# Moving PSUM reads of a soft-MoE kernel from VectorE to ScalarE, with the addition one block later

## The chip, the cores and the metric

The kernel runs on one core of a Trainium2 chip. The metric is the device time of one execution in microseconds. Three timed runs of the kernel before gave 395.83 (median), 395.76 and 396.35.

## The reference

Causal attention over 8 batches of 12 heads (448 positions, 64 channels each) is followed by a soft mixture of experts over all 3584 tokens of 768 channels. Cut to what matters:

```python
attn = softmax(where(causal, q @ k.T / 8, -1e9));  x = attn @ v      # per batch and head
x = x.transpose(0, 2, 1, 3).reshape(3584, 768)
logits = x @ phi                                  # 32 slots
d = exp(logits - logits.max(0));  d /= d.sum(0)   # softmax over the tokens
slot_input = d.T @ x                              # 32 x 768, "dispatch"
slot_out[e] = relu(slot_input[e] @ w1[e]) @ w2[e] # 8 experts of 4 slots
c = softmax(logits, axis=1);  out = c @ slot_out
```

The softmax of d runs over all tokens. So the kernel keeps a running maximum and a running sum over the batches, and rescales the summed slot input each time by a factor `al`.

## The kernel before, in words

The work is a loop over 48 pairs of heads (`block(p)`, p from 0 to 46, then `last_block`); six pairs make a batch. Every engine keeps the order in which the program issues its instructions (`_InOrder`, line 57). Because of that helper, all instructions of the profile stand under line 67, and one goes by the names of the tiles.

Scores need two passes. The first pass (`scores1_all`, lines 285 to 287) computes the transposed scores of one head into one of three PSUM score tiles `s_` (line 96; 128 partitions by 1024 columns of float32, which is two banks of 512 columns). Its first matmul writes the causal mask (`tri`) into columns 512 to 703. VectorE takes maxima over the scores (`max_keys`, `r<-s` and `r<-r`), TensorE transposes them (`max_row`, into `rt`, or for the second head of a pair into the last 128 columns of a score tile), VectorE reduces them to a row (`mr`), and GpSimd spreads it into an operand (`max_spread`, `r<-mr`). A second pass (`scores2`, `s<-r,k`) subtracts the maxima and adds the low parts of the operands; ScalarE takes exponentials of a whole tile (`exps`, `pt<-s`), and TensorE multiplies them by the values (`attv_pair`, `po<-va,pt`). VectorE divides by the sums (`norm`; its part 2, `x<-po,sm`, runs at the start of the next block), TensorE transposes x (`xtrans`) and ScalarE copies it out (`xcopy`).

The running mixture of experts is strewn over the blocks by the remainder p % 6 (`m6`), lines 645 to 673. At the end of a block the score tile of the pair's second head, `m = s_[(a + 1) % 3]` with a = 2 p, is free, and TensorE writes into it:

- in blocks with remainder 3, 5 and 1 the logits of a pair of head pairs (j = 0, 2, 4) into columns 0 to 127; `logits_t` (lines 444 to 446) adds them on VectorE to the tile `lt`. For j = 0 the second operand is `mk`, a constant that holds 0, and -1e30 where the batch has no tokens (448 of 512 rows are real);
- in remainder 2 the transposed weights and logits of the batch before, copied out by VectorE;
- in remainder 3, 4 and 0 (from p = 7 on) the products of a dispatch: 128 columns, 256 columns (both at column 512) and 384 columns (at column 0). `dispatch_b` (lines 486 to 489) rescales the running slot input `si` by `al` and adds the products in one VectorE instruction.

The transposed maxima of the next head go into columns 896 to 1023 of the same tile m, and their reduction `mr` precedes `logits_t` and `dispatch_b` on VectorE. Two score passes later, in the next block, the tile m takes the first-pass scores of head a + 4 (`scores1_all(a' + 2)` of the next block p + 1, a' = 2 p + 2). So its first matmul, the mask, has to wait until m has been read.

The order on each engine around the change of blocks is then: TensorE: attention times values, logits or dispatch, the transposed maxima, `xtrans`, the second pass of the next block's first head, the mask and the first pass into m, the second pass of the second head, the first pass of another head, attention times values. VectorE: `norm` parts 0 and 1 (`sm<-po` and the reciprocal `sm<-sm`), `mr`, `logits_t`, `dispatch_b`, `norm` part 2, then the maxima. ScalarE: casts of the operands, the factors of the running softmax (`al`, `lt<-run_m`, `run_z`), the next exponential.

After the attention the experts' weights, 50 MB in all of which a part is loaded ahead, are streamed through tiles that lie over dead tiles of the attention (`wt1`, line 781); a pad (`PAD`, lines 39 and 777) sets where they begin.

Of the kernel before, what the change touches and what calls it, by code (L numbers as in the profile page):

```python
# [9 lines left out]
F32 = mybir.dt.float32  # L10
F32R = mybir.dt.float32r
BF16 = mybir.dt.bfloat16
AF = mybir.ActivationFunctionType
ALU = mybir.AluOpType
# [3 lines left out]
P = 128  # L18
# [16 lines left out]
RES, TW1, LATE2 = 24, 11, 4  # L35

HT = 2
WN, PAD = 1536, 192
WARM = (2, 3, 3)
START = (9, 6, 2, 4)  # L40

# [41 lines left out]
def attention_soft_moe(ctx: ExitStack, tc: tile.TileContext, qk, va, phi, w, out):  # L83
    nc = _Core(tc)
    const = ctx.enter_context(tc.tile_pool(name="const", bufs=1, side="left"))
# [30 lines left out]
    ltn = moe.tile([P, P + 1], F32, name="lt")  # L116
    lt = ltn[:, 0:P]
    gs = moe.tile([P, P], F32, name="gs")
    mk = moe.tile([P, P], F32, name="mk")

    st = {"w": 0}
# [14 lines left out]
    def loads_v(p, eng=nc.sync):  # L136
        if p < NPAIR:
            eng.dma_start(out=va_[p % 2], in_=va[p])
# [30 lines left out]
    def load_w(n):  # L169
        if n < len(order):  # L170
            t = wtiles[order[n]] = slot(n, f"w{n}")
            q, g, c = place(n), (n + 2) // 4, WN * ((n + 2) % 4)
            if n < RES or n == NBUF or q >= RES + LATE2:
                nc.sync.dma_start(out=t, in_=w[g, :, c:c + WN])
            elif 4 <= q < RES and n > NBUF:
                if q % 4 == 3:
                    nc.sync.dma_start(out=group(n), in_=w[g])
            elif n % 2:
                t = group(n)
                nc.sync.dma_start(out=t[:, 2 * WN:] if q < RES else t, in_=w[g, :, c - WN:c + WN])  # L180
# [54 lines left out]
    def cast_q(p, hs=slice(0, 2)):  # L235
        if p < NPAIR:
            nc.scalar.activation(out=qd[:, hs], in_=st["raw", 0, p][:, hs], func=AF.Copy)
# [97 lines left out]
    def scores2(i, cs):  # L335
        if i >= NHD:
            return
        p, h = divmod(i, 2)
        s = st["s", i]
        k2 = k2_  # L340
        for c in cs:
            o, w, m = KS * h + P * c, S - CQ0[c], min(P, KS - P * c)
            nc.tensor.matmul(s[0:m, SCOL[c]:SCOL[c] + w], k2[:, o:o + m],
                             r2[:, h, CQ0[c]:S], start=False, stop=True, skip_group_check=True)

    def exps(i):
        if i < NHD:
            nc.scalar.activation(out=pt_[i % 2][:, 0:1024], in_=st.pop(("s", i)), func=AF.Exp, scale=SCALE)
# [49 lines left out]
    def x_of(p):  # L398
        if p % 3 == 0:
            xn = st["xn", p // 3] = x_[p // 3 % XB]  # L400
            for k in range(3):
                st["x", p + k] = xn[:, :, P * k:P * k + P]
        return st["x", p]

    def norm(p, k):
        if k == 0:
            sm = st["sm", p] = moe.tile([P, NQ], F32, tag="sm", name=f"sm{p}", bufs=2)
            nc.vector.tensor_scalar(out=sm, in0=po2[:, :, HD], scalar1=EPS, scalar2=None, op0=ALU.add)
        elif k == 1:
            nc.vector.reciprocal(out=st["sm", p], in_=st["sm", p])  # L410
        else:
            x, sm = x_of(p), st.pop(("sm", p))
            m = NCH - 1
            nc.vector.tensor_tensor(out=x[:, 0:m].rearrange("p c (h d)->p h c d", h=2),
                                    in0=po2[:, 0:2 * m, 0:HD].rearrange("p (h c) d->p h c d", h=2),
                                    in1=sm[:, 0:2 * m].rearrange("p (h c)->p h c", h=2).unsqueeze(3)
                                    .to_broadcast([P, 2, m, HD]), op=ALU.mult)
            for h in range(2):
                a = AW * h
                nc.vector.tensor_scalar(out=x[0:AW, m, HD * h:HD * h + HD], in0=po2[a:a + AW, 2 * m, 0:HD],  # L420
                                        scalar1=sm[a:a + AW, 2 * m:2 * m + 1], scalar2=None, op0=ALU.mult)
# [21 lines left out]

    def logits_t(j, g):

        nc.vector.tensor_tensor(out=lt, in0=g, in1=lt if j else mk, op=ALU.add)

    def logits_b(b):

# [36 lines left out]
    def dispatch_b(b, hf, sp, sl=slice(0, 384)):  # L486
        s = si[:, 384 * hf + sl.start:384 * hf + sl.stop]
        nc.vector.scalar_tensor_tensor(out=s, in0=s, scalar=st["al", b][:, 0:1], in1=sp[:, 0:sl.stop - sl.start],
                                       op0=ALU.mult, op1=ALU.add)
# [8 lines left out]
    phis = [const.tile([P, 3, NSLOT], F32, tag="ph", name=f"phi{hf}", bufs=2) for hf in range(2)]  # L498
    run_m = [const.tile([P, 1], F32, name=f"run_m{i}") for i in range(2)]
    run_z = const.tile([P, 1], F32, name="run_z")  # L500
    lg = const.tile([P, NB, NCH, NSLOT], F32, name="lg")


# [16 lines left out]
    copy_k2(0, h0)  # L520
    sub_k(0, h0, nc.vector)
    nc.vector.memset(pob, 0.0)
    for t, v in ((mk, 0.0), (mk[96:P, 64:P], -1.0e30), (ltn[:, P:P + 1], -1.0e30), (run_m[1], 1.0e30), (run_z, 0.0)):
        nc.vector.memset(t, v)
    sub_q(0, h0)
    scores1_all(0)
# [37 lines left out]
    def block(p):  # L564
        a, b = 2 * p, p // 6 - 1
        m6 = p % 6
        if p + 1 < NPAIR:
            loads_v(p + 1, nc.sync if p + 1 < NPAIR - 1 else nc.scalar)
        if p % 2 and p < 44 or p in (16, 30):
            load_w(st["w"])  # L570
            st["w"] += 1

        if p:
            norm(p - 1, 2)
        scores2(a, range(NCH))
        exps(a)
        if p == 0:
            copy_k2(0, h1)
            cast_q(1, h1)
            warm(START[3], pob)  # L580
            max_row(1, 0)
            max_row(1, 1)
            max_spread(1)
            sub_k(1, h1, nc.vector)
        elif p > 1:
            xcopy(p - 2)
            if p == NPAIR - 2:
                sub_q(p + 1, h0)
        scores1_all(a + 2)
        if p == 0:  # L590
            warm(START[2], pob)
        for k in range(3):
            max_keys(a + 2, k)
        if p == 0:
            cast_k(2, h0)
        scores2(a + 1, range(NCH))
        exps(a + 1)
        if p == 0:
            cast_k(2, h1)
        scores1_all(a + 3)  # L600
        if m6 == 2 and p > 6:
            logits_b(b)
        max_keys(a + 3, 0)
        late_k = p == 1
        if p == 1:
            sub_q(2, h0)
            sub_k(3, h0)
            sub_q(2, h1)
            load_qk(4, 0)
        elif p:  # L610
            sub_k(p + 2, h0 if late_k else slice(0, 2))
            if not late_k:
                load_qk(p + 4, 1)
            sub_q(p + 1, h1 if p == NPAIR - 2 else slice(0, 2))
            load_qk(p + 3, 0)
        else:
            sub_q(1, h0)
            sub_q(1, h1)
            load_qk(3, 0)
            sub_k(2, h0)  # L620
        copy_k2(p + 1)
        if m6 == 2 and p > 6:
            logits_d(b, lt)
        if p:
            cast_k(p + 3)
            cast_q(p + 2)
        else:
            cast_q(2)
            cast_k(3)
        if m6 == 3 and p > 6:  # L630
            logits_al(b)
        elif m6 == 4 and p > 6:
            logits_n(b)
        attv_pair(p)
        max_row(a + 2, 1)
        max_spread(a + 2)
        if p == 0:
            sub_k(2, h1)
            load_qk(4, 1)
        for k in (1, 2):  # L640
            max_keys(a + 3, k)
        for k in range(2):
            norm(p, k)

        m = s_[(a + 1) % 3]
        parts = []
        if m6 in (1, 3, 5) and p > 1:
            j = (m6 + 3) % 6
            logits_a(b if m6 == 1 else p // 6, (j, j + 1), m[:, 0:P])
        elif m6 == 2 and p > 6:  # L650
            logits_e(b, m, 0)
        if m6 == 3 and p > 6:
            parts = [(b, 0, slice(0, P), 512)]
        elif m6 == 4 and p > 6 and p < NPAIR - 2:
            parts = [(b, 0, slice(P, 3 * P), 512)]
        elif m6 == 0 and p > 6:
            parts = [(b - 1, 1, slice(0, 3 * P), 0)]
        for d, hf, sl, o in parts:
            dispatch_a(d, hf, m[:, o:o + sl.stop - sl.start], sl)
        max_row(a + 3, 0, to=m[:, 1024 - P:1024])  # L660
        max_row(a + 3, 1)
        if m6 == 2 and p > 6:
            logits_e(b, m, 1)
        max_spread(a + 3)
        if late_k:
            sub_k(p + 2, h1)
            load_qk(p + 4, 1)
        if m6 in (1, 3, 5) and p > 1:
            logits_t(j, m[:, 0:P])
        for d, hf, sl, o in parts:  # L670
            dispatch_b(d, hf, m[:, o:o + sl.stop - sl.start], sl)
        if p:
            xtrans(p - 1)

# [31 lines left out]
    for c in range(NCH):  # L706
        n = P if c < NCH - 1 else AW
# [207 lines left out]
    n = NBUF  # L915
# [93 lines left out]
```

## Time and profile before

| what | value |
|---|---|
| median of three timed runs | 395.83 us |
| the profiled execution's own time | 396.08 us |
| its span from first to last instruction | 394.4 us |
| granted TensorE clock, mean | 0.979 |
| attention loop, from the first exponential to the last | about 10 to 297 us |
| bytes moved | 119.17 MB, mean 302 GB/s |

The profile comes from one execution. Each row of a group gives the line, engine, operation, the tile written and the tiles read, the shapes, the count, busy time and mean duration of one. Rows of the timeline begin with the start and the duration in us, and end with the idle time of the engine before them and what ended it, where there was any. PE is TensorE's matmuls, PEld its weight loads, DVE VectorE, ACT ScalarE, POOL GpSimd, SP the queue that issues most DMAs. Ends of matmuls are modelled.

### The profile page before, as it was taken

To read this page: it belongs to the slowest core of one execution; us is meant where nothing else is said; L and a number is where in the kernel's file an instruction comes from. 1 tells how busy PE (TensorE), PEld (TensorE's weight loads), DVE (VectorE), ACT (ScalarE), POOL (GpSimd) and SP (SyncE) were. 2 spreads that over 40 slices of the span, in tenths; PEclk is the share of its full clock that TensorE was granted. 3 is DMA by queue.
4 is the path that set the end of the run, shared out by engine and by line. 5 is a ranking of instruction groups with operands and counts; after the bars stand their busy time and mean duration, and the time that the engine had idled before them with its cause. 6 is when DMAs were issued, how large, how long until landed. Compare 5 with 4: busy or idle time off the path is not lost.

```text
span 394.4 us, 13997 instructions
## 1 busy us (share of the span) xinstructions
PE 366.3 (93%) x5763; PEld 293.9 (75%) x5763; DVE 295.2 (75%) x835; ACT 282.9 (72%) x397; POOL 256.5 (65%) x215
## 2 busy tenths in 40 slices
PE   7899999999999999999999999999999989988940
PEld 3689889888988998898889888988986544533420
DVE  7887889888888888898888988888886675342550
ACT  5888899898898898888988988888864012431440
POOL 5998899898898888898988988889860000000000
PEclk9999999999999999999999999999999999998985
DMA  7868877788898788777997877887579999999996
GB/s 250 277 229 281 288 288 237 251 273 274 274 318 272 244 270 300 257 246 248 307 323 256 286 240 249 275 287 250 183 246 399 422 431 428 429 421 419 433 429 295
DMA packets 28720, 119.17 MB, mean 302 GB/s; under 512 B 3440, under 2 KB 3952, under 8 KB 26480
## 3 DMA queue, kind: packets, MB, share of 16 engines
q1 hardware_dynamic: 28512, 118.01, 83.2%
q8 instruction: 45, 0.74, 0.7%
q10 hardware_dynamic: 144, 0.27, 0.2%
q14 instruction: 19, 0.16, 0.1%
HBM read 107.25 MB, written 11.01 MB: 300 GB/s over the span
## 4 chain that ended last, share of the span: by engine, by line
PE 67%; DMA 9%; POOL 9%; DVE 5%; ACT 4%; issue 2%; SPq 0%; POOLq 0%; DVEq 0%; ACTq 0%
PE s L67 34%; PE po L67 20%; DMA w<-in_w_dram 8%; POOL r L67 6%; PE xm L67 4%; POOL ks L67 3%; PE so L67 2%; PE e L67 2%; PE pp L67 2%; PE rt L67 2%; DMA kraw<-in_qk_dram 1%; ACT qd L67 1%; DVE lm L67 1%; DVE lg L67 1%; ACT w L67 1%
## 5 line engine op out<-in xcount | busy, mean ns | idle before, releaser
L67 DVE TRANSPOSE_TENSOR_REDUCE r<-s 128x32 f32<-128x1024 f32 x96 | 119.5, 1245 | 7.7 <-PE s L67 4.9
L67 ACT ACTIVATE pt<-s 128x1024 f32<-128x1024 f32 x96 | 98.8, 1029 | 31.0 <-PE s L67 24.0
L67 PEld LDWEIGHTS po<-va,pt 128*64 128x64 f32 x3008 | 102.3, 138 | 11.8 <-issue 11.3
L67 PE MATMUL po<-va,pt 128*64 128x65 f32 x3008 | 109.2, 224 | 0.0
L67 POOL TENSOR_TENSOR r<-qraw,qd 64x896 fp32r<-64x896 f32 (+1 forms) x50 | 99.4, 1989 | 1.9 <-ACT qd L67 1.8
L67 POOL TENSOR_TENSOR ks<-kraw,ks 64x896 fp32r<-64x896 f32 (+1 forms) x48 | 89.7, 1870 | 4.1 <-ACT ks L67 0.5
L67 POOL TENSOR_SCALAR_AFFINE_SELECT r<-mr 14x448 fp32r<-14x448 f32 x96 | 61.6, 643 | 32.9 <-DVE mr L67 28.6
L67 PE MATMUL s<-qd,ks 128*66 128x64 f32 (+3 forms) x384 | 80.6, 321 | 0.0
L67 PE MATMUL s<-r,k 128*128 128x448 f32 (+3 forms) x384 | 65.2, 291 | 2.7 <-POOL r L67 2.7
L67 PEld LDWEIGHTS s<-r,k 128*128 128x128 f32 (+1 forms) x384 | 59.3, 176 | 8.6 <-POOL r L67 5.9
L67 PEld LDWEIGHTS s<-qd,ks 128*128 128x128 f32 (+1 forms) x384 | 52.5, 183 | 2.1 <-issue 0.9
L67 ACT ACTIVATE ks<-kraw 128x896 fp32r<-128x896 f32 (+1 forms) x49 | 45.0, 920 | 5.6 <-DMA kraw<-in_qk_dram 4.4
L67 ACT ACTIVATE k<-ks 64x896 fp32r<-64x896 f32 (+1 forms) x49 | 45.8, 936 | 1.2
L67 ACT ACTIVATE qd<-qraw 128x896 fp32r<-128x896 f32 (+1 forms) x48 | 44.6, 929 | 0.9 <-POOL r L67 0.7
L67 PE MATMUL s<-tri,identb 128*128 128x192 bf16 x192 | 39.6, 270 | 0.6
L67 DVE TENSOR_REDUCE r<-r 128x16 f32<-128x32 f32 x192 | 33.7, 176 | 5.0
L67 DVE TENSOR_REDUCE mr<-s 14x32 f32<-14x128 f32 x47 | 13.1, 279 | 21.4 <-ACT qd L67 14.8
L67 PE MATMUL xm<-ident,x 128*128 128x128 f32 x188 | 28.3, 273 | 0.0
L67 ACT ACTIVATE xts<-xm 128x512 f32<-128x512 f32 x46 | 27.2, 591 | 0.4 <-PE xm L67 0.4
L67 DVE TENSOR_SCALAR x<-po,sm 64x64 f32<-64x64 f32 x94 | 25.9, 276 | 0.7
L67 DVE COPY w<-pp 128x384 f32<-128x384 f32 x28 | 14.5, 553 | 15.4 <-PE pp L67 15.3
L67 DVE TENSOR_TENSOR x<-po,sm 128x384 f32<-128x384 f32 x47 | 25.2, 537 | 0.0
(151 smaller groups left out, 397.9 us busy)
## 6 DMA issues: line engine op xcount, KB each, us to landing
w<-in_w_dram SPq DMA_DIRECT2D x34, 768.0 KB, 6.7
kraw<-in_qk_dram SPq DMA_DIRECT2D x46, 448.0 KB, 4.4
qraw<-in_qk_dram SPq DMA_DIRECT2D x46, 448.0 KB, 4.5
w<-in_w_dram SPq DMA_DIRECT2D x5, 3072.0 KB, 25.0
va<-in_va_dram SPq DMA_DIRECT2D x47, 260.0 KB, 4.8
out_dram<-w SPq DMA_DIRECT2D x7, 1536.0 KB, 12.6
w<-in_w_dram SPq DMA_DIRECT2D x5, 1536.0 KB, 11.2
qk<-in_qk_dram SPq DMA_DIRECT2D x2, 448.0 KB, 7.1
```

The lines of the kernel that those rows point to most:

```text
L67: return self._tc.keep_in_program_order(op(*args, **kwargs))
```

## The change

For the first pair of a batch (j = 0) `logits_t` no longer adds a constant on VectorE; ScalarE copies the logits out of the score tile into `lt`. The -1e30 of the missing tokens is written into `lt` by VectorE in the next block (remainder 4). Of a dispatch of 256 or 384 columns VectorE sums only the first 128 out of PSUM. ScalarE copies the other 128 or 256 columns into a new buffer `scr` in SBUF, and VectorE sums that copy into `si` in the next block, behind the reciprocal. The constant `mk` is no longer filled at the start; the tile stays, since the tail uses it. The pad shrinks from 192 to 128 columns, and `scr` takes 256 columns.

```diff
--- before.py
+++ after.py
@@ -35,7 +35,7 @@
 RES, TW1, LATE2 = 24, 11, 4
 
 HT = 2
-WN, PAD = 1536, 192
+WN, PAD = 1536, 128
 WARM = (2, 3, 3)
 START = (9, 6, 2, 4)
 
@@ -443,7 +443,10 @@
 
     def logits_t(j, g):
 
-        nc.vector.tensor_tensor(out=lt, in0=g, in1=lt if j else mk, op=ALU.add)
+        if j:
+            nc.vector.tensor_tensor(out=lt, in0=g, in1=lt, op=ALU.add)
+        else:
+            nc.scalar.activation(out=lt, in_=g, func=AF.Copy)
 
     def logits_b(b):
 
@@ -498,6 +501,7 @@
     phis = [const.tile([P, 3, NSLOT], F32, tag="ph", name=f"phi{hf}", bufs=2) for hf in range(2)]
     run_m = [const.tile([P, 1], F32, name=f"run_m{i}") for i in range(2)]
     run_z = const.tile([P, 1], F32, name="run_z")
+    scr = const.tile([P, 2 * P], F32, name="scr")
     lg = const.tile([P, NB, NCH, NSLOT], F32, name="lg")
 
 
@@ -520,7 +524,7 @@
     copy_k2(0, h0)
     sub_k(0, h0, nc.vector)
     nc.vector.memset(pob, 0.0)
-    for t, v in ((mk, 0.0), (mk[96:P, 64:P], -1.0e30), (ltn[:, P:P + 1], -1.0e30), (run_m[1], 1.0e30), (run_z, 0.0)):
+    for t, v in ((ltn[:, P:P + 1], -1.0e30), (run_m[1], 1.0e30), (run_z, 0.0)):
         nc.vector.memset(t, v)
     sub_q(0, h0)
     scores1_all(0)
@@ -641,6 +645,10 @@
             max_keys(a + 3, k)
         for k in range(2):
             norm(p, k)
+        for d, hf, sl in st.pop("rest", ()):
+            dispatch_b(d, hf, scr, sl)
+        if m6 == 4:
+            nc.vector.memset(lt[96:P, 64:P], -1.0e30)
 
         m = s_[(a + 1) % 3]
         parts = []
@@ -668,7 +676,11 @@
         if m6 in (1, 3, 5) and p > 1:
             logits_t(j, m[:, 0:P])
         for d, hf, sl, o in parts:
-            dispatch_b(d, hf, m[:, o:o + sl.stop - sl.start], sl)
+            n = sl.stop - sl.start - P
+            dispatch_b(d, hf, m[:, o:o + P], slice(sl.start, sl.start + P))
+            if n:
+                nc.scalar.activation(out=scr[:, 0:n], in_=m[:, o + P:o + P + n], func=AF.Copy)
+                st["rest"] = ((d, hf, slice(sl.start + P, sl.stop)),)
         if p:
             xtrans(p - 1)
 
```

## The prediction

> **What bounds the kernel now.** I read the page first, then the chain of waits, then the timeline of single blocks, one engine at a time. On the page TensorE is busy almost throughout, and the transfer rate shows where another limit begins:
>
> ```profile
> PE 366.3 (93%) x5763; PEld 293.9 (75%) x5763; DVE 295.2 (75%) x835; ACT 282.9 (72%) x397; POOL 256.5 (65%) x215
> GB/s 250 277 229 281 288 288 237 251 273 274 274 318 272 244 270 300 257 246 248 307 323 256 286 240 249 275 287 250 183 246 399 422 431 428 429 421 419 433 429 295
> ```
>
> The last ten slices (about 100 us, the experts) run at some 420 to 430 GB/s, against 183 to 323 before. Their loads wait for tiles of the attention to die, so whatever the attention gains or loses is carried to the end unchanged. All edits lie in the attention's blocks, and there TensorE works in program order. The question is thus where TensorE waits at the change of blocks.
>
> A block change without a dispatch sum (into block 12; time zero is the first second-pass score, 83.04), VectorE and then TensorE:
>
> ```profile
> 82.99 0.28 DVE L67 TENSOR_REDUCE mr<-s 14x32 f32<-14x128 f32 x1 [0.51 <-PE s L67]
> 84.52 1.25 DVE L67 TRANSPOSE_TENSOR_REDUCE r<-s 128x32 f32<-128x1024 f32 x1
> ...
> 83.04 0.72 PE L67 MATMUL s<-r,k 128*128 128x448 f32 x4
> 83.60 0.26 PE L67 MATMUL s<-tri,identb 128*128 128x192 bf16 x1
> ...
> 85.67 0.92 PE L67 MATMUL po<-va,pt 128*64 128x65 f32 x24
> 86.42 0.27 PE L67 MATMUL rt<-ident,r 128*64 128x128 f32 x1
> ```
>
> The mask matmul (`tri`) opens the next scores in the score tile that the old block has just used. It starts at 0.56, the transposing maximum (`r<-s`) 0.92 later at 1.48, attention times values (`po`) at 2.63, the transposition `rt` 0.75 after that. Now the same after a 384-wide sum (into block 13, zero 89.17):
>
> ```profile
> 89.33 0.59 DVE L67 SCALAR_TENSOR_TENSOR si<-si,al,s 128x384 f32<-128x384 f32 x1
> 89.85 0.54 DVE L67 TENSOR_TENSOR x<-po,sm 128x384 f32<-128x384 f32 x1
> ...
> 90.92 1.25 DVE L67 TRANSPOSE_TENSOR_REDUCE r<-s 128x32 f32<-128x1024 f32 x1
> 92.20 0.40 DVE L67 TENSOR_REDUCE r<-r 128x16 f32<-128x32 f32 x2
> ...
> 89.17 0.71 PE L67 MATMUL s<-r,k 128*128 128x448 f32 x4
> 89.97 0.24 PE L67 MATMUL s<-tri,identb 128*128 128x192 bf16 x1
> ...
> 91.95 0.92 PE L67 MATMUL po<-va,pt 128*64 128x65 f32 x24
> 92.75 0.29 PE L67 MATMUL rt<-ident,r 128*64 128x128 f32 x1
> ```
>
> The mask starts at 0.80, 0.05 after the sum ends (0.75). So the sum is on the path. `po` starts at 2.78, only 0.15 late, because it also waits for something else when the mask is early: po = max(2.63, mask + 1.98). VectorE is late too: x to r<-s is 1.07, r<-s to the end of r<-r 1.68, and rt comes 0.15 after that, 0.80 behind po instead of 0.75. After rt everything follows TensorE.
>
> Two more rows, of the chain of waits:
>
> ```profile
> DVE mr L67 <- ACT qd L67: 14.8, 24, 0.7
> ACT pt L67 <- DVE si L67: 4.4, 5, 0.9
> ```
>
> `mr` does not read qd, and the exponential `pt` does not read si. The page names the last event of a counter waited for. So `mr`, a VectorE read of a score tile, waits on ScalarE's counter (ScalarE's work on that tile is an exponential's read), and the exponential waits on VectorE's (there a maximum's read). Also, the mask above writes columns 512 to 703 and still waited for a sum that reads columns 0 to 383. I read from this that the program orders the engines' accesses to one score tile whole, reads behind reads included.
>
> **The change part by part.** There are three kinds of block change, by the page of the tile si and the conditions in the code: A, after p % 6 = 3, seven times (9 to 45); B, after 4, six times (10 to 40; one of the seven 256-wide sums is the last block's and unchanged); C, after 0, six times (12 to 42).
>
> ```profile
> L67 DVE SCALAR_TENSOR_TENSOR si<-si,al,s x20: 325/458/593, 71.3 to 295.5; 128x128 f32<-128x128 f32 x7, 128x256 f32<-128x256 f32 x7, 128x384 f32<-128x384 f32 x6
> ```
>
> New on ScalarE are PSUM copies of 128 (A, B) and 256 columns (C). The nearest rows are such copies in the tail; for the handover between the engines I take 0.04, the gap between these two instructions:
>
> ```profile
> L67 ACT ACTIVATE mk<-e 128x128 f32<-128x128 f32 x1 | 0.3, 277 | 0.2 <-PE e L67 0.2
> L67 ACT ACTIVATE xta<-e 128x256 f32<-128x256 f32 x1 | 0.4, 377 | 0.0
> ...
> 310.95 0.29 DVE L67 TENSOR_TENSOR lg<-lg,lm 128x128 f32<-128x128 f32 x1
> ...
> 311.28 0.31 ACT L67 ACTIVATE lg<-lg 128x128 f32<-128x128 f32 x1 [1.71 <-DVE lg L67]
> ```
>
> Kind A, as it is (zero 70.97):
>
> ```profile
> 70.92 0.28 DVE L67 TENSOR_REDUCE mr<-s 14x32 f32<-14x128 f32 x1 [0.74 <-ACT qd L67]
> 71.13 0.27 DVE L67 TENSOR_TENSOR lt<-s,mk 128x128 f32<-128x128 f32 x1
> 71.33 0.33 DVE L67 SCALAR_TENSOR_TENSOR si<-si,al,s 128x128 f32<-128x128 f32 x1
> 71.58 0.54 DVE L67 TENSOR_TENSOR x<-po,sm 128x384 f32<-128x384 f32 x1
> ...
> 70.97 0.71 PE L67 MATMUL s<-r,k 128*128 128x448 f32 x4
> 71.71 0.24 PE L67 MATMUL s<-tri,identb 128*128 128x192 bf16 x1
> ...
> 73.69 0.92 PE L67 MATMUL po<-va,pt 128*64 128x65 f32 x24
> ```
>
> Three VectorE reads of the tile run back to back, overlapping. The change puts ScalarE between them: mr ends 0.23, copy 0.27 to 0.55, sum 0.59 to 0.92, mask 0.97 (was 0.74). po becomes 0.97 + 1.98 = 2.95 (was 2.72). x, 0.25 behind the sum's start, goes from 0.61 to 0.84, so rt from 0.61 + 1.07 + 1.68 + 0.15 = 3.51 to 3.74. All is 0.23 later: 7 x 0.23 = 1.61 us. Behind the waiting copy on ScalarE stands only the next exponential, due at 0.74; behind the waiting sum on VectorE stand x and the maxima, counted here.
>
> Kind B, as it is (zero 77.04), with ScalarE's last work before the copy:
>
> ```profile
> 77.19 0.46 DVE L67 SCALAR_TENSOR_TENSOR si<-si,al,s 128x256 f32<-128x256 f32 x1
> ...
> 77.04 0.72 PE L67 MATMUL s<-r,k 128*128 128x448 f32 x4
> 77.70 0.24 PE L67 MATMUL s<-tri,identb 128*128 128x192 bf16 x1
> ...
> 79.67 0.92 PE L67 MATMUL po<-va,pt 128*64 128x65 f32 x24
> ...
> 76.98 0.38 ACT L67 ACTIVATE run_z<-run_z,bs,al 128x1 f32<-128x1 f32 x1
> 77.79 1.03 ACT L67 ACTIVATE pt<-s 128x1024 f32<-128x1024 f32 x1 [0.44 <-PE s L67]
> ```
>
> The halved sum ends at 0.15 + 0.33 = 0.48, the copy runs 0.52 to 0.80, the mask starts 0.85 (was 0.66), po 2.83 (was 2.63). VectorE's x comes at 0.41, but r<-s needs mask + 0.92 = 1.77, so rt = 1.77 + 1.68 + 0.15 = 3.60 (was, from x at 0.54, 3.44): +0.16, 6 times 0.96 us. The exponential at 0.75 is pushed by at most the copy's last 0.05, which the late mask hides.
>
> Kind C: sum 0.16 to 0.49, copy of 256 0.53 to 0.91, mask 0.96 (was 0.80), r<-s 1.88, rt 3.71 (was 3.58): +0.13, 6 times 0.78 us. The exponential starts some 0.1 later; the mask is later still, so this costs nothing more.
>
> The deferred sums (six of 128, six of 256 columns) and eight small fills go between the reciprocal and mr, where VectorE idles 0.51 to 0.74 (the brackets of the mr rows). The 256-wide row is 0.46; I cost them at nothing. If that cover were gone they would delay mr, and with it GpSimd's spread:
>
> ```profile
> 82.13 0.64 POOL L67 TENSOR_SCALAR_AFFINE_SELECT r<-mr 14x448 fp32r<-14x448 f32 x1
> ...
> 82.28 0.20 DVE L67 RECIPROCAL sm<-sm 128x7 f32<-128x7 f32 x1
> ...
> 11.68 0.68 DVE L67 TENSOR_TENSOR ks<-kraw,ks 64x448 fp32r<-64x448 f32 x1
> ...
> 11.95 0.92 POOL L67 TENSOR_SCALAR_AFFINE_SELECT r<-mr 14x448 fp32r<-14x448 f32 x1
> ```
>
> At 11.95 the spread took 0.92 instead of 0.64, begun while VectorE combined two SBUF operands; the deferred sums are such instructions, and one ready at 82.48 would meet a spread that runs to 82.77. If it sat that out (0.29) and then held VectorE 0.38, mr would come at 83.15, 0.16 late after the 256-wide ones: 6 x 0.16 = 1.0 us, my upper end for this term. I take zero, since these blocks become 0.13 to 0.16 longer while the spread stays. The Trainium skill, SBUF — State Buffer, "Who interferes with whom", says that a VectorE instruction with two SBUF inputs and a GpSimd instruction that reads SBUF exclude each other; by it the sum would be 1.0 higher at most, and the stretched spread agrees.
>
> The start's two fills of mk go away beside other waits (VectorE's next work waits for scores). The new buffer takes 1 KB and the pad gives back 256 bytes; by their sizes the late weight tiles lie over the same early tiles as before, so their loads wait for the same work: nothing. Sum: 1.61 + 0.96 + 0.78 = 3.35 us. The profiled execution took 396.08 (span 394.4 and 1.68 around it), 0.25 above the median of 395.83; it would become 399.4, the median 399.2.
>
> **The rivals.** First, faster: reads are not ordered against reads. Then the copies run beside VectorE: A's mask returns to 0.56 and rt to 2.63 + 0.75 = 3.38 (-0.13), B's rt to 3.38 (-0.06, the copy done by 0.59 after run_z), C's likewise (-0.20): 0.91 + 0.36 + 1.20 = 2.47 us, 393.4. It decides wherever a copy starts before VectorE's sum ends. For it: the idle ScalarE; against it: the two rows of waits. Chance 0.08.
>
> Second, order by bank only. A's copy (columns 0 to 127) and sum (512 to 639) lie in different halves, so A gains 0.91 while B and C lose 1.74: 396.7. Against it: the mask of columns 512 up waiting for a read of 0 to 383. Chance 0.06. The Trainium skill, PSUM — Partial Sum Buffer, "PSUM bank collisions raise a hardware error", asks for just this: two engines, readers too, must be kept apart in one bank and quadrant, while different banks run clean. By that rule the time is this rival's; no run here shows an unordered pair.
>
> Third, GpSimd's lock costs its full 1.0 on top: 400.2. Chance 0.08. The forecast itself has 0.78.
>
> **How the numbers follow.** The predicted time is the forecast's, 399.2. With handovers of 0.02 to 0.08 and copies of 0.26 to 0.31 each event moves by 0.08 at most, 19 times 1.5 us; with the lock's part I give 397.6 to 400.8. That leaves out the first two rivals, 0.14. A measurement here can tell about 0.2%, 0.8 us. Slower holds the forecast and the third rival and a little of the second: 0.88; same holds most of the second: 0.04; faster is the first: 0.08.
>
> **What would show it.** The mask after A, B, C at 0.97, 0.85, 0.96 from the first second-pass score; in A the sum starting behind ScalarE's copy; in B and C the copy starting behind the sum; blocks one longer by 0.23, 0.16, 0.13. The forecast is wrong if the copies start before VectorE's read has ended, or if the tail does not shift with the attention.

## The result and the profile after

The changed kernel is slower: a median of 400.99 us in four runs (400.84 to 401.35) against 396.01 (395.76 to 396.35) for the kernel before in as many, a ratio of 1.0124 with a 95% interval of 1.0112 to 1.0137. The forecast was 399.2 within 397.6 to 400.8. The direction is the forecast's, the size lies 0.2 us outside its range.

From the page after, the row of busy times and the transfer rate in 40 slices:

```profile
PE 367.8 (92%) x5763; PEld 294.3 (74%) x5763; DVE 296.0 (74%) x845; ACT 289.4 (73%) x417; POOL 256.5 (64%) x215
GB/s 254 285 199 285 291 278 244 255 253 274 259 327 242 257 273 271 252 240 250 313 306 239 278 230 263 307 247 229 201 228 379 407 439 431 427 426 412 434 426 331
```

TensorE has the same 5763 matmuls and 1.5 us more busy time; the span grew from 394.4 to 399.1. So TensorE waits more. VectorE got no relief worth the name (296.0 instead of 295.2 us, ten instructions more) and ScalarE 6.5 us of new work.

Now the three kinds of block change, timeline of the changed kernel: A into block 16 (time zero 108.75), B into block 11 (78.05), C into block 13 (90.44). The last TensorE row of each is the start of the block behind it.

```profile
108.70 0.28 DVE L67 TENSOR_REDUCE mr<-s 14x32 f32<-14x128 f32 x1 [0.73 <-ACT qd L67]
109.32 0.35 DVE L67 SCALAR_TENSOR_TENSOR si<-si,al,s 128x128 f32<-128x128 f32 x1 [0.34 <-ACT lt L67]
110.65 1.25 DVE L67 TRANSPOSE_TENSOR_REDUCE r<-s 128x32 f32<-128x1024 f32 x1
...
109.01 0.28 ACT L67 ACTIVATE lt<-s 128x128 f32<-128x128 f32 x1 [0.24 <-DVE mr L67]
...
108.75 0.72 PE L67 MATMUL s<-r,k 128*128 128x448 f32 x4
109.72 0.24 PE L67 MATMUL s<-tri,identb 128*128 128x192 bf16 x1 [0.25 <-DVE si L67]
...
115.05 0.60 PE L67 MATMUL s<-r,k 128*128 128x448 f32 x2
```

```profile
78.20 0.33 DVE L67 SCALAR_TENSOR_TENSOR si<-si,al,s 128x128 f32<-128x128 f32 x1
...
79.92 1.25 DVE L67 TRANSPOSE_TENSOR_REDUCE r<-s 128x32 f32<-128x1024 f32 x1 [0.43 <-ACT pt L67]
...
78.62 0.28 ACT L67 ACTIVATE scr<-s 128x128 f32<-128x128 f32 x1 [0.33 <-DVE si L67]
...
78.05 0.71 PE L67 MATMUL s<-r,k 128*128 128x448 f32 x4
78.95 0.24 PE L67 MATMUL s<-tri,identb 128*128 128x192 bf16 x1 [0.19 <-ACT scr L67]
...
81.75 0.29 PE L67 MATMUL rt<-ident,r 128*64 128x128 f32 x1
...
84.31 0.45 PE L67 MATMUL s<-r,k 128*128 128x448 f32 x1
```

```profile
90.60 0.33 DVE L67 SCALAR_TENSOR_TENSOR si<-si,al,s 128x128 f32<-128x128 f32 x1
...
92.42 1.25 DVE L67 TRANSPOSE_TENSOR_REDUCE r<-s 128x32 f32<-128x1024 f32 x1 [0.54 <-PE s L67]
...
91.02 0.38 ACT L67 ACTIVATE scr<-s 128x256 f32<-128x256 f32 x1 [0.71 <-DVE si L67]
...
90.44 0.71 PE L67 MATMUL s<-r,k 128*128 128x448 f32 x4
91.45 0.24 PE L67 MATMUL s<-tri,identb 128*128 128x192 bf16 x1 [0.29 <-ACT scr L67]
...
96.82 0.45 PE L67 MATMUL s<-r,k 128*128 128x448 f32 x1
```

In A the copy begins 0.03 behind mr (109.01 behind 108.98), the sum 0.03 behind the copy, the mask 0.05 behind the sum, at 0.97 as forecast. In B and C the copy begins 0.09 behind the sum (78.62 behind 78.53, 91.02 behind 90.93), the mask follows at 0.90 and 1.01 (forecast 0.85 and 0.96), and the maximum `r<-s` comes 0.97 behind the mask, where A shows 0.93. In B the transposition `rt` starts at 3.70 instead of 3.60. The blocks take 6.30, 6.26 and 6.38 us, against 6.07 and 6.00 (by rows of the prediction) and 6.14 before (6.143 in the trace's nanoseconds, from 89.17):

```profile
95.32 0.45 PE L67 MATMUL s<-r,k 128*128 128x448 f32 x1
```

That is +0.23, +0.26 and +0.24. Seven, six and six times make 1.61 + 1.56 + 1.44 = 4.61 us. The table of waits after names the new chain (waiting engine and tile, releaser, us in total, times, longest):

```profile
ACT scr L67 <- DVE si L67: 5.9, 11, 0.8
PE s L67 <- ACT scr L67: 3.1, 12, 0.4
ACT lt L67 <- DVE mr L67: 2.4, 8, 0.6
DVE si L67 <- ACT lt L67: 2.4, 7, 0.3
```

So ScalarE waits for VectorE's read, TensorE for ScalarE's, and in A VectorE for ScalarE's: readers of one score tile stand in line. The first two rivals needed copies that run beside VectorE's reads; of the 20 copies in the trace none does. The third needed deferred sums that meet GpSimd's spread: here they begin when at most 0.13 us of a spread is left, and take their 0.30 and 0.43 us.

### The profile page after: what moved, and what is told of

Same layout as the page of the kernel before. It is cut to its first block, busy times and chain, and to the rows that moved or that the text cites. A ratio compares the mean times of both kernels' runs of the same rounds, so it can differ in the third digit from the quotient of the medians.

```text
span 399.1 us, 14014 instructions
## 1 busy us (share of the span) xinstructions
PE 367.8 (92%) x5763; PEld 294.3 (74%) x5763; DVE 296.0 (74%) x845; ACT 289.4 (73%) x417; POOL 256.5 (64%) x215
## 4 chain that ended last, share of the span: by engine, by line
PE 56%; ACT 11%; POOL 10%; DMA 7%; DVE 7%; issue 5%; DVEq 0%; ACTq 0%; POOLq 0%
PE s L67 29%; PE po L67 14%; DMA w<-in_w_dram 7%; POOL r L67 7%; ACT qd L67 4%; POOL ks L67 3%; PE xm L67 3%; ACT k L67 3%; PE e L67 2%; PE so L67 2%; PE pp L67 2%; ACT pt L67 2%; DVE si L67 1%; DVE mr L67 1%; DVE lm L67 1%
```

## The experiments

All changes are to the kernel before or to the changed kernel. "Behind A" is the length of the block behind kind A, median of those in the profile, and so on; the loop runs from the start of block 1 to that of block 47. What lies ahead of it is called the start, what follows the tail.

| kernel | behind A | behind B | behind C | loop, us | ratio to before |
|---|---|---|---|---|---|
| before | 6.07 | 6.00 | 6.14 | 277.05 | |
| changed | 6.30 | 6.27 | 6.38 | 282.33 | 1.0124 (1.0112 to 1.0137) |
| e1 A only | 6.30 | 6.00 | 6.14 | 278.67 | 1.0039 (1.0026 to 1.0051) |
| e2 B and C only | 6.06 | 6.27 | 6.37 | 280.66 | 1.0082 (1.0069 to 1.0094) |
| e3 fills back | 6.30 | 6.27 | 6.38 | 281.85 | 1.0122 (1.0108 to 1.0136) |
| e4 reads ahead of mr | 6.19 | 6.04 | 6.28 | 279.90 | 1.0075 (1.0061 to 1.0088) |
| e5 ScalarE first | 6.06 | 6.30 | 6.41 | 280.53 | 1.0093 (1.0079 to 1.0106) |
| e6 ScalarE alone | 6.06 | 6.06 | 6.17 | 277.60 | 1.0021 (1.0013 to 1.0029) |
| e7 no deferred sums | 6.07 | 6.27 | 6.38 | 280.12 | 1.0083 (1.0070 to 1.0096) |
| e8 VectorE copies | 6.07 | 6.07 | 6.20 | 278.45 | 1.0029 (1.0018 to 1.0041) |
| e9 changed, again | 6.30 | 6.27 | 6.38 | 282.43 | one run: 401.38 us |
| e10 before, again | 6.06 | 6.01 | 6.14 | 277.05 | one run: 395.83 us |
| e11 one wait | 6.07 | 5.99 | 6.10 | 276.92 | 0.9997 (0.9987 to 1.0007) |
| e12 A, B, C by ScalarE | 5.99 | 6.13 | 6.10 | 277.19 | 1.0040 (1.0027 to 1.0053) |
| e13 the same, fill moved, pad | 5.99 | 5.99 | 6.10 | 276.66 | 1.0002 (0.9993 to 1.0011) |
| e14 without the pad | 5.99 | 5.99 | 6.10 | 276.66 | 1.0031 (1.0019 to 1.0043) |

**e1, kind A alone.** The split of the dispatch is taken out again; the start's fills and the pad are those of before.

```diff
-            n = sl.stop - sl.start - P
-            dispatch_b(d, hf, m[:, o:o + P], slice(sl.start, sl.start + P))
...
+            dispatch_b(d, hf, m[:, o:o + sl.stop - sl.start], sl)
```

> Only the logits copy (kind A) is changed; the dispatch sums, the constant mk's fills and the pad are as before. Theory T (each read of a score tile that passes between VectorE and ScalarE costs a handover that TensorE waits out): mask 0.97 and the next block 0.23 longer, seven times, so +1.6 us; with the tail giving back part of it, as after the whole change, +1.2 to +1.6, ratio 1.003 to 1.004. Rival S (the loss beyond 3.35 us lies at the start and in single interruptions, not in the blocks): the same +1.6 here, but with a start at 17.07 and no interruptions. Rival F (copy overlaps VectorE's sum): -0.9 us.

Measured 1.0039, 1.5 us, and a loop 1.62 longer: 7 x 0.23. The forecast's term for A was 1.61.

**e2, kinds B and C alone.** `logits_t` and the start's fills as before, and no fill of -1e30 in the loop.

```diff
-        if j:
-            nc.vector.tensor_tensor(out=lt, in0=g, in1=lt, op=ALU.add)
-        else:
-            nc.scalar.activation(out=lt, in_=g, func=AF.Copy)
+        nc.vector.tensor_tensor(out=lt, in0=g, in1=lt if j else mk, op=ALU.add)
```

> Only the split dispatch (kinds B and C) is changed; the logits and the start are as before. T with the handovers that the trace after shows (0.09 rather than 0.04, and the maximum 0.97 rather than 0.92 behind the mask): blocks longer by 0.26 (six times) and 0.24 (six times), +3.0 us, ratio 1.007 to 1.008. T with the sizes of the prediction: +1.74 us, ratio 1.0044. If kind A and kinds B and C add up, this ratio and that of the logits alone multiply to the whole change's, 1.0124, less what the start and single interruptions took.

Measured 1.0082, 3.2 us: the larger sizes hold, the prediction's 1.74 us for B and C do not. (The loop is 3.61 longer: 3.0 in the twelve blocks, and 0.6 in single delays in blocks 17 and 24, of which more under e9.) e1 and e2 together make 1.0121; the two parts add up.

**e3, the fills at the start put back.**

> The changed kernel with the two fills of mk at the start put back. If the start's 0.38 us comes from the fills that went, the first maximum on VectorE is back at 6.36 and the ratio to before falls from 1.0124 to 1.0114. If it is chance or the position of the instructions, the start's delay comes and goes without regard to the fills, and the ratio stays at 1.0124 within 0.001. The single interruptions of VectorE (blocks 10, 17, 24) show in the same places if they belong to the program, in others or not at all if they do not.

The ratio stays, 1.0122. The first maximum comes at 5.96 here, earlier than before the change, but block 0 is then 0.5 longer and block 1 begins at 17.17. Blocks 10, 17 and 24 are undisturbed, and block 31 is 0.20 longer instead. So neither the start nor the interruptions hang on the fills as work; e9 tells more.

**e4, the reads ahead of mr, all on VectorE.**

```diff
+        if m6 in (1, 3, 5) and p > 1:
+            logits_t(j, m[:, 0:P])
+        for d, hf, sl, o in parts:
+            dispatch_b(d, hf, m[:, o:o + sl.stop - sl.start], sl)
         max_row(a + 3, 1)
```

> The kernel before with one move: the logits' addition and the dispatch sums are issued on VectorE ahead of the reduction mr instead of behind it (no ScalarE copy, nothing deferred). T: the score tile's last reader is then mr, the mask starts at 0.56 after A and B; A gains 0.13 (seven times), B 0.06 (six times), C between 0.06 and 0.20 (the 384-wide sum may push mr and GpSimd's spread by up to 0.2, which gives some of it back): -1.3 to -2.5 us, ratio 0.994 to 0.997. Rival (mr is on the path through GpSimd's spread and the second pass, so that what goes ahead of it is lost again): between no change and +2 us.

Measured 1.0075, 3.0 us slower: my expectation failed and its rival holds. Timeline of e4 into block 16 (zero 108.54):

```profile
108.04 0.31 PE L67 MATMUL s<-ident,r 128*76 128x128 f32 x1
...
108.45 0.29 DVE L67 TENSOR_TENSOR lt<-s,mk 128x128 f32<-128x128 f32 x1 [0.70 <-ACT qd L67]
108.66 0.34 DVE L67 SCALAR_TENSOR_TENSOR si<-si,al,s 128x128 f32<-128x128 f32 x1
108.92 0.27 DVE L67 TENSOR_REDUCE mr<-s 14x32 f32<-14x128 f32 x1
...
109.26 0.64 POOL L67 TENSOR_SCALAR_AFFINE_SELECT r<-mr 14x448 fp32r<-14x448 f32 x1 [1.38 <-DVE mr L67]
```

The reads start at -0.09, hardly earlier than mr did (-0.05): the transposed maxima go into the same tile behind the products, and the reads come after those too (`s<-ident,r` ends at -0.19). So mr is pushed to 0.38, GpSimd's spread from 0.30 to 0.72, and with it the second pass of the second head. VectorE's idle time ahead of mr is not there to be filled with reads of this tile.

**e5, ScalarE's copy ahead of VectorE's sum (B and C alone).**

```diff
+            if n:
+                nc.scalar.activation(out=scr[:, 0:n], in_=m[:, o + P:o + P + n], func=AF.Copy)
+                st["rest"] = ((d, hf, slice(sl.start + P, sl.stop)),)
             dispatch_b(d, hf, m[:, o:o + P], slice(sl.start, sl.start + P))
-            if n:
-                nc.scalar.activation(out=scr[:, 0:n], in_=m[:, o + P:o + P + n], func=AF.Copy)
-                st["rest"] = ((d, hf, slice(sl.start + P, sl.stop)),)
```

> Kinds B and C alone, with the two readers in the other order: ScalarE's copy ahead of VectorE's 128-wide sum. Theory W (a handover is about 0.03; what made B and C dearer is that the copy there waits on two engines' counters, and the maximum r<-s behind it too, each second wait one instruction of about 0.05 on the path): in this order copy and maximum wait on one each; mask 0.97 after B and 1.08 after C, r<-s 0.93 behind it, blocks 0.28 and 0.25 longer than before, +3.2 us, ratio 1.008. Theory H (every handover between VectorE and ScalarE costs 0.09): mask 1.07 and 1.18, r<-s 0.97 behind it, blocks longer by 0.43 and 0.41, +5.0 us, ratio 1.0127.

The list of instructions of the programs has a counter for each engine, and names for each instruction the engines whose counters it waits for. It gave theory W, and stands here in short form. In the changed kernel A's copy waits for one engine, B's for two, and so does the maximum behind B; a second wait takes a semaphore instruction of its own ahead, which the timeline does not show (first A's two, then B's):

```
L67 ACTIVATE lt<-s_80 128x128 [waits DVE_49]
L67 TENSOR_REDUCE r_90<-s_80 128x2x16 [waits PE_49]
...
L67 ACTIVATE scr<-s_79 128x128 [waits DVE_49,PE_49]
L67 TENSOR_REDUCE r_90<-s_79 128x2x16 [waits PE_49,Activation_49]
```

The Trainium skill, Perfetto Trace Analysis, "Identifying Dependency Chains", says that an instruction which waits on several engines may get semaphore instructions put ahead of it; these lists agree. The trace has that instruction too, with its nanoseconds. In A the copy begins 0.034 behind the end of `mr`. In all twelve events of B and C the semaphore instruction begins 0.03 behind the end of VectorE's sum, and the copy 0.094 behind it. So the handover is as short behind a sum as behind `mr`, and the second wait adds 0.06. In e5 each of the two waits for one engine. Into block 11 (zero 77.50):

```profile
77.45 0.28 DVE L67 TENSOR_REDUCE mr<-s 14x32 f32<-14x128 f32 x1 [0.51 <-ACT qd L67]
78.08 0.35 DVE L67 SCALAR_TENSOR_TENSOR si<-si,al,s 128x128 f32<-128x128 f32 x1 [0.34 <-ACT scr L67]
79.41 1.25 DVE L67 TRANSPOSE_TENSOR_REDUCE r<-s 128x32 f32<-128x1024 f32 x1
...
77.76 0.28 ACT L67 ACTIVATE scr<-s 128x128 f32<-128x128 f32 x1
...
78.47 0.24 PE L67 MATMUL s<-tri,identb 128*128 128x192 bf16 x1 [0.26 <-DVE si L67]
```

Both handovers are 0.03 to 0.04, the mask is at 0.97, the maximum 0.94 behind it: W within a hundredth, and H (0.09 for each handover, mask 1.07) falls. The blocks are 0.30 and 0.27 longer, where W had 0.28 and 0.25 and H 0.43 and 0.41. The time, 1.0093, is nearer to W's 1.008 than to H's 1.0127; this program's loop also begins 0.45 later than that of before.

**e6, ScalarE alone copies (B and C), and e11, the same with one wait.** In e6 the whole 256 or 384 columns go through ScalarE and VectorE reads nothing behind mr. e11 adds (second diff) a copy of one column, where VectorE is idle, so that VectorE has waited for ScalarE before the maximum comes. In both the buffer is 384 columns wide, a tile of the tail shares it, and the pad is 0.

```diff
-            dispatch_b(d, hf, m[:, o:o + P], slice(sl.start, sl.start + P))
+                n += P
+                nc.scalar.activation(out=scr[:, 0:n], in_=m[:, o:o + n], func=AF.Copy)
+                st["rest"] = ((d, hf, sl),)
```

```diff
             norm(p - 1, 2)
+        if "rest" in st:
+            nc.vector.tensor_copy(out=dum, in_=scr[:, 0:1])
```

> Kinds B and C alone, with no VectorE read behind mr: ScalarE copies all 256 or 384 columns, and the whole sum comes in the next block. W: the copies start 0.03 behind mr, 0.26 to 0.65 and 0.26 to 0.76; mask 0.70 and 0.81; the maximum is not told by VectorE's own reads, so it may wait on two counters: blocks up to 0.06 and 0.03 longer than before, 0 to +0.6 us, ratio 1.000 to 1.0015. H: copies start at 0.32, blocks 0.12 and 0.09 longer, +1.3 us, ratio 1.003. If the deferred sums (256 and 384 columns now) cost, block 6 n + 5 and 6 n + 1 behind them begin late, by up to 0.2 each.

> The kernel in which ScalarE copies all of kinds B and C, plus one tiny VectorE copy of a single column of scr, which waits for ScalarE ahead of the maximum r<-s while VectorE has nothing to do; the maximum then waits on TensorE alone. W: mask 0.70 and 0.80 as there, but r<-s 0.92 to 0.93 behind it instead of 0.97, at 1.61 and 1.73; blocks 6.01 and 6.12 instead of 6.06 and 6.17, so 0.6 us less than there and within 0.2 us of before, ratio 0.999 to 1.001. If the 0.05 is not the second wait: 6.06 and 6.17, ratio 1.0014 to 1.002.

Timelines into block 11, of e6 (zero 76.64) and of e11 (76.69):

```profile
78.30 1.25 DVE L67 TRANSPOSE_TENSOR_REDUCE r<-s 128x32 f32<-128x1024 f32 x1 [0.47 <-PE s L67]
...
76.90 0.39 ACT L67 ACTIVATE scr<-s 128x256 f32<-128x256 f32 x1
...
76.64 0.72 PE L67 MATMUL s<-r,k 128*128 128x448 f32 x4
77.33 0.24 PE L67 MATMUL s<-tri,identb 128*128 128x192 bf16 x1
```

```profile
77.91 0.16 DVE L67 COPY dum<-scr 128x1 f32<-128x1 f32 x1
78.28 1.25 DVE L67 TRANSPOSE_TENSOR_REDUCE r<-s 128x32 f32<-128x1024 f32 x1 [0.22 <-PE s L67]
...
76.95 0.38 ACT L67 ACTIVATE scr<-s 128x256 f32<-128x256 f32 x1
...
76.69 0.72 PE L67 MATMUL s<-r,k 128*128 128x448 f32 x4
77.39 0.24 PE L67 MATMUL s<-tri,identb 128*128 128x192 bf16 x1
```

The mask is at 0.69 to 0.70 in both, but the maximum 0.97 behind it in e6 and 0.89 in e11, and the blocks are 6.06 and 5.99. One tiny instruction more, which takes the second wait away from the path, gives 0.07 for each event. The trace has the same price: from the end of TensorE's last score to the maximum it is 0.106 with the semaphore instruction between (e6) and 0.037 without (e11). A's 0.93 behind the mask is more than e11's 0.89 although A waits for one engine, because in A VectorE itself works on x until 0.03 before the maximum. The ratios are 1.0021 and 0.9997: e11's lies where it was expected, e6's above its 1.000 to 1.0015, though its blocks are as expected. With both second waits off the path, moving the reads to ScalarE costs nothing any more; it also gains nothing that can be measured.

**e7, the deferred sums left out, and e8, VectorE makes the copy.**

```diff
-        for d, hf, sl in st.pop("rest", ()):
-            dispatch_b(d, hf, scr, sl)
+        st.pop("rest", None)
```

```diff
-                nc.scalar.activation(out=scr[:, 0:n], in_=m[:, o + P:o + P + n], func=AF.Copy)
+                nc.vector.tensor_copy(out=scr[:, 0:n], in_=m[:, o + P:o + P + n])
```

> Kinds B and C alone, with the deferred sums left out (two thirds of the slot input are then missing from the output). If the deferred sums cost nothing, the ratio is that of kinds B and C alone, 1.0082, within 0.001. If GpSimd's spread and the sums hold each other up (the prediction's third rival), 1.0 us less, 1.0057.

> Kinds B and C alone, with VectorE in place of ScalarE for the copy of the second part: the same split, deferral and buffer, no handover. W and H alike: mask 0.73 after B and 0.83 after C, one wait for each instruction, blocks 0.04 to 0.08 longer, +0.3 to +0.8 us, ratio 1.001 to 1.002. If instead the split or the deferral itself costs (and not the handovers), +2.5 to +3.2 us as in kinds B and C alone.

e7 shows 1.0083 against e2's 1.0082, and its blocks behind B and C are as long as e2's: the twelve deferred sums cost nothing in the changed kernel, and rival three falls for it. (The loop of e7 is 0.54 shorter, but that is e2's delays in blocks 17 and 24; its start is 0.62 later.) e8 shows 1.0029; the blocks are longer by 0.07 and 0.06, 0.78 us together, and a single interruption in each of blocks 17 and 24 adds 0.59. So split, buffer and deferral cost a quarter of what e2 costs in the blocks (0.78 of 3.0); the rest is the way through ScalarE. The ratio lies above the expected 1.001 to 1.002 because of the two interruptions.

**e9 and e10, both kernels profiled again.**

> The changed kernel once more, for a second profile. What belongs to the change repeats: blocks longer by 0.23, 0.26 and 0.24, an attention loop some 4.6 us longer than before. If the late start (block 1 at 17.45 instead of 17.07), the single interruptions of VectorE in blocks 10, 17 and 24 (0.66 us together) and the shorter tail (99.3 instead of 100.3) are chance of one execution, they come out otherwise here; if they belong to the program, the same.

> The kernel before once more, for a second profile: the loop of 277.05 us from block 1 to block 47 repeats within 0.1; the start (17.07) and the tail (100.25) may differ by some tenths, if they are chance of one execution.

The single interruptions repeat to the hundredth: blocks 10, 17 and 24 take 6.67, 6.48 and 6.22 (6.67, 6.47 and 6.21 the first time). The reduction mr of block 10 in the first and in the second execution of the changed kernel:

```profile
71.70 0.28 DVE L67 TENSOR_REDUCE mr<-s 14x32 f32<-14x128 f32 x1 [1.10 <-PE xm L67]
```

```profile
71.73 0.28 DVE L67 TENSOR_REDUCE mr<-s 14x32 f32<-14x128 f32 x1 [1.10 <-PE xm L67]
```

So these belong to the program, not to chance. But they do not belong to the mechanism: e3 has one in block 31 instead, e2 and e8 in blocks 17 and 24, e13 and e14 in 17, e12 in 24, and e1, e5 and e7 nowhere in the loop. It is no wait that the trace shows: the semaphore instruction ahead of block 10's mr ends at 71.28, and mr begins 0.42 behind it instead of the usual 0.05.

The trace does tell where they strike. Count VectorE's records in it from the first, semaphore instructions included. The late instruction is number 192 in block 10, 320 in block 17 and 448 in block 24 of the changed kernel, 320 and 448 in e2 and e8, 576 in e3, 320 in e13 and e14, 448 in e12: always 64 past a multiple of 128, in all 14 cases. So every 128 instructions VectorE's stream has a place that can be late, by 0.18 to 0.38 us in these cases, and an edit that adds or removes instructions decides what stands there. Behind a wait that is long anyway it costs nothing; at mr, or at the sum or the addition behind it, it makes the block longer. The fetching of instructions would fit (the profile lists transfers of a kind `instruction`), but no run tests it.

Block 1 begins at 17.45 and 17.46 in the changed kernel, at 17.07 and 17.22 in the kernel before. The tail is 99.3 and 99.8 us against 100.3 and 99.9: shorter by 0.93 in the first pair of profiles and by 0.08 in the second, so most of that is one execution's.

**e12 to e14, everything through ScalarE.** In A one copy takes 2 x 128 columns out of both halves of the tile into a buffer that holds `scr` and `lt`; B and C go as in e11. In e12 the fill of -1e30 stays behind the deferred sum; in e13 and e14 it stands at the start of the block, behind the one-column copy. The pad is 0 in e12 and e14 and 448 in e13.

```diff
+            if m6 == 3 and parts:
+                nc.scalar.activation(out=big[:, 2 * P:4 * P].rearrange("p (h s) -> p h s", h=2),
+                                     in_=m.rearrange("p (h s) -> p h s", h=2)[:, :, 0:P], func=AF.Copy)
+                st["rest"], parts = ((b, 0, slice(0, P), 2 * P),), []
```

> As the one before, and kind A too by ScalarE alone: logits and dispatch products lie in the two halves of the score tile, and one copy of 2 x 128 columns takes both; the whole dispatch sum comes in the next block. The copy's two destinations share one buffer. W: copy 0.26 to 0.65, mask 0.70 (before 0.74), r<-s 1.63 (before 1.67): block 6.02 instead of 6.07, seven times 0.05; with B and C at 6.01 and 6.12 the sum is -0.3 to -0.5 us, ratio 0.998 to 1.000: about the kernel before. Theory H or a copy over two banks that is slower: 1.001 or more.

> As the kernel in which ScalarE makes all copies (A, B and C), with the fill of -1e30 moved to where VectorE waits for scores (behind the one-column copy), and the pad of the tail grown by 448 columns, since the shared buffer moved the attention's tiles under the late weights. Theory L (the 128-wide deferred sum stood still until GpSimd's spread had ended, 0.52 instead of 0.30, and the fill behind it pushed mr by 0.12): with the fill gone from there, mr is back at -0.05 to 0.00, blocks behind B 5.99 to 6.04 instead of 6.11 to 6.13; loop 276.2 to 276.5 us, against 277.05 before. With a tail of 99.8 to 100.3 the time is 0.5 to 1.0 us below before, ratio 0.9975 to 0.999. If the late mr there had another cause (the shared buffer's waits), blocks stay 6.11 and the ratio is 1.000 or more.

> The same without the grown pad. If the place of the late weights over the attention's tiles made the tail of the kernel with all copies on ScalarE 0.8 us longer (101.0 instead of 100.25 in its profile), it is again some 0.8 longer than with the grown pad, ratio 1.000 to 1.002; if that was chance of one program's layout, both come out alike within 0.3 us.

A gains what was expected and a little more, 5.99 instead of 6.07. But in e12 the block behind B is 6.13, and the ratio 1.0040 where 0.998 to 1.000 was expected. The lock of the prediction's third rival shows itself there: GpSimd's spread and the deferred 128-wide sum of the changed kernel, behind kind B, and then of e12, behind kind A:

```profile
83.67 0.30 DVE L67 SCALAR_TENSOR_TENSOR si<-si,al,scr 128x128 f32<-128x128 f32 x1
...
83.13 0.64 POOL L67 TENSOR_SCALAR_AFFINE_SELECT r<-mr 14x448 fp32r<-14x448 f32 x1
```

```profile
75.94 0.52 DVE L67 SCALAR_TENSOR_TENSOR si<-si,al,lt 128x128 f32<-128x128 f32 x1
76.51 0.11 DVE L67 MEMSET lt<- 32x64 f32 x1
76.66 0.28 DVE L67 TENSOR_REDUCE mr<-s 14x32 f32<-14x128 f32 x1
...
75.69 0.64 POOL L67 TENSOR_SCALAR_AFFINE_SELECT r<-mr 14x448 fp32r<-14x448 f32 x1
```

In the changed kernel the sum meets the last 0.10 of the spread and takes 0.30; in e12 it meets the last 0.39 and takes 0.52, to 0.13 behind the spread's end. The Trainium skill, SBUF — State Buffer, "Who interferes with whom", has just this exclusion, for a VectorE instruction with two SBUF inputs and a GpSimd instruction that reads SBUF; the rows of e12 agree. The fill behind the sum then puts mr 0.12 late. e13 takes the fill away from there: its sums still take 0.50 to 0.53, but mr is back at -0.05 and the block at 5.99. So the lock by itself costs no time here; it took the idle time that the fill needed. e13 and e14 have the same loop, 276.66 (with a single interruption of 0.35 in block 17), but e14's tail is 100.96 us in its profile, as e12's 101.01, and e13's 100.14: it fits that the shared buffer, which moves the attention's tiles under the late weights, costs some 0.8 us, and the pad gives it back. Their profiles also differ by 0.79 in the start (block 1 at 16.68 and 17.46), which the pad should not touch; I do not know why. The best of the three, e13, is at 1.0002: level with the kernel before, though its loop is 0.39 shorter and 0.9975 to 0.999 was expected. No version beat the kernel before.

## Why the prediction was wrong in size

**The mechanism was right.** Readers of one score tile go in the program's order, whatever their columns and engine; the mask waits for the last of them; A behaves as forecast at each step (mask 0.97, block +0.23, e1: 1.62 us in the loop for 1.61). Deferred sums (e7) and fills (e1, where the loop grows by the seven blocks alone) cost nothing. The rivals by which copies would run beside VectorE's reads fall by the waits and by e5.

**The step that failed** is the one under kinds B and C: "the halved sum ends at 0.48, the copy runs 0.52 to 0.80, the mask starts 0.85 ... but r<-s needs mask + 0.92". I took the handover, 0.04, from a pair in the tail, and 0.92 from a block in which only VectorE had read the tile. Both are right where an instruction waits for one engine, as in A. In B and C the copy stands behind VectorE's sum and TensorE's products, the maximum behind TensorE's scores and ScalarE's copy: two counters each. That put 0.05 on the copy and 0.05 on the maximum, by the terms of the sum (0.09 for 0.04, and 0.97 for 0.92), so B cost 0.26 instead of 0.16 and C 0.24 instead of 0.13. Six times 0.10 and six times 0.11 are 1.26 us: B and C measure 1.56 + 1.44 = 3.00 where I had 1.74. e5 (other order, one wait each), e11 (second wait moved into idle time) and the semaphore instructions in the trace show it to be the second wait and not the way between the engines. That mis-sizing accounts for 4.61 us in the blocks where the forecast had 3.35.

My range allowed "0.08 at most" for an event; it knew handovers of different length, but not that an instruction may need two of them.

**The rest**, 4.98 by the medians less 4.61, is small and does not belong to the mechanism: by the first pair of profiles a start 0.38 later, single interruptions of 0.66 in blocks 10, 17 and 24, and a tail 0.93 shorter, with the 4.61 together 4.72 us, where the two profiled executions are 4.76 apart. The prediction put start and pad at nothing and said the whole shift would reach the end. In the second pair the start is 0.25 later, the interruptions are the same, and the tail is 0.08 shorter, so there the shift does reach the end. The interruptions come from what the edit put at every 128th place of VectorE's stream, a term that the prediction did not have; what sets the start stays open.

## What to carry to other kernels

Moving a read to an idle engine helps only if the program lets the two engines read side by side; look first at how many readers stand in line for the tile, and whether the next writer waits for the last. When an edit puts another engine into that line, count for every instruction on the path the engines it must wait for: one was nearly free here (0.03 to 0.05 us), a second cost 0.06 to 0.07 more, and a tiny instruction in idle time that does the second wait earlier took it off the path. Before filling an idle gap with work, see what the gap waits for (e4) and what another engine does beside it (e12). And before a few tenths of a microsecond are put down to a change, see whether single blocks are late and where in the engine's stream.

## What the runs showed that I had not expected

A two-input VectorE sum beside a running GpSimd spread is not slowed in proportion. With 0.10 of overlap the 128-wide sum took its usual 0.30 us, with 0.31 (e8) 0.44, with 0.39 (e12) 0.52. In the last two it ended 0.13 behind the spread's end. The wider sums do the same: 256 columns end 0.26 to 0.27 behind the spread (e11: 0.65 to 0.67 instead of the usual 0.43), 384 columns 0.40 behind it. So what has to wait for the spread is some 0.13 us for each 128 columns; the remaining 0.17 of the instruction goes on beside it, and a short overlap is free.

And one program repeats its own odd delays: block 10's mr waited 1.10 us in both executions of the changed kernel, in a block where no other kernel shows such a delay, and there alone mr is the 192nd of VectorE's records.
